# Moving matrix transposes from the tensor engine to DMA in a linear-attention-plus-MLP kernel, with a reordered load and a second load gate

## The chip, the cores and the metric

The kernel runs on one core of one Trainium2 chip. The metric is the device time of one execution in microseconds (us), for the slowest core (here the only one). Executions of one kernel on this chip usually agree within a few tenths of a per cent (the kernel before: 290.83 to 291.37 us in the 20 runs of two groups; in a third group one run of 11 took 292.80 us), so a kernel is timed several times, in rounds that alternate with the kernel before. Engines are named as in the profile: PE is the tensor engine's matmuls, PEld its weight loads (they overlap PE: 158.9 us busy beside PE's 279.8 in a span of 289.2 us), DVE the vector engine, ACT the scalar engine, POOL the general engine (it issues the loads here), SP the sync engine (it issues stores and DMA transposes here).

## The reference, cut to what matters

```python
# q, k, v: [8 batches, 8 heads, 576 rows, 64]
kv  = einsum('bhsd,bhse->bhde', k, v)            # one 64x64 matrix for each batch and head
out = einsum('bhsd,bhde->bhse', q, kv)
x   = out / sqrt(mean(out**2, -1) + 1e-6) * g_norm   # over the 64 of a head
x   = x.transpose(0, 2, 1, 3).reshape(8, 576, 512)
# layer norm, MLP 512 -> 2048 -> 512, residual
xn  = (x - mean(x)) / sqrt(var(x) + 1e-6) * g_ln
return x + maximum(xn @ w_ch1, 0) @ w_ch2
```

## The kernel before

All matmuls are in bf16. A batch of 576 rows is four "main" tiles of 128 rows and a rest of 64 rows; the rests of two batches make one tile more. For each tile the kernel computes q times kv, normalises the result to x on ACT and DVE, turns x (the MLP needs it with d_model on the partitions), and runs the two products of the MLP, mm1 (`w1`) and mm2 (`w2`). Both q and x have to be turned. Where time is short they are turned by four PE matmuls against the identity, into PSUM, with a copy by ACT; elsewhere one DMA does it.

```python
def load_batch(b, after=None):
    if after is not None:
        nc.gpsimd.tensor_copy(gate, after)     # POOL waits for one element: holds the loads back
    load(k_in[b % NB], k, b)                   # two DMAs each, 256 KB and 320 KB
    load(v_in[b % NB], v, b)
    load(q_in[b % NB], q, b)

def turn_q(b, j, pool, tag):                   # one of the five groups of q, on PE
    tp = pool.tile([128, HP, 128], bf16, tag=tag, name="tp")
    for hp in range(HP):
        nc.tensor.transpose(tp[:, hp, :n], q_ps[b][:n, j, ...], identity[:n, :n])
    nc.scalar.copy(qts[b][:, j, :, :n], tp[:, :, :n])

def turn_q_dma(b):                             # all five groups, by DMA (batches 2 to 7)
    q_p = kv_in.tile(...)
    nc.vector.tensor_copy(q_p.rearrange("p j h d -> p h j d"), q_in[b % NB])
    q_t = qt_pool.tile(...)
    nc.sync.dma_start_transpose(q_t..., q_p...)
    qts[b] = q_t

def kv_of(b):                                  # k^T v: 40 small matmuls
    ...
```

The MLP's matmuls are cut into slots, and an agenda says at which slot other work is put between them: `at(slot, function)`; `tick()` in the MLP loops advances the slot and runs what is due. One slot is about 0.86 us of matmuls: late in the kernel before, with nothing between them, the 16 slots of mm2 of a batch took 13.82 us (244.02 to 257.84 us). Slots 0 to 15 are mm1 of batch 0, 16 to 31 mm2 of batch 0, 32 to 47 mm1 of batch 1, and so on. `plan_tile(s, make, turn_at, on_pe)` plans a tile's attention at slot s and the turning of its x at slot turn_at, on PE or by DMA.

```python
load_w2(0); load_w2(1)
load_batch(1)
load_w2(2); load_w2(3)
...
fill(18)                                       # matmuls on zeros while the first loads come in
...
at(21, lambda: kv_of(1))
q_turns(23, 1)                                 # batch 1: copy of q, then turn_q of all 5 groups on PE
for j, s, tn in ((0, 24, 30), (1, 27, 34), (2, 31, 38), (3, 35, 42)):
    plan_tile(s, lambda j=j: main_tile(1, j), tn, True)
at(36, lambda: kv_of(2))
at(36.5, lambda: turn_q_dma(2))
for j, s, tn in ((0, 44, 50), (1, 48, 54), (2, 53, 61), (3, 58, 67)):
    plan_tile(s, lambda j=j: main_tile(2, j), tn, j > 1)      # tiles 2 and 3 on PE
for b in range(3, B):
    s = 32 * b
    at(47 if b == 3 else s - 60,
       lambda b=b: load_batch(b, qts[b - 1][:1, J, HP - 1, 127:]))  # not before q of b-1 is turned
    d = -41 if b == 3 else -45
    at(s + d, lambda b=b: kv_of(b))
    at(s + d + 1.7, lambda b=b: turn_q_dma(b))
    for j in range(J):
        o = s + d + (10 if b == 3 else 13) + 5 * j
        plan_tile(o, lambda b=b, j=j: main_tile(b, j), o + 6, False)
    ...
```

The cut places are marked with dots.

## Time and profile before

The kernel before takes 290.84 us (median of three runs, 290.82 to 290.87). What matters of its profile:

| | before |
|---|---|
| span of the profiled execution | 289.2 us |
| PE busy | 279.8 us, 97% of the span |
| ACT and DVE busy | 155.4 and 149.8 us |
| chain that ended last | 91% PE |
| transposes on PE of batch 1's q, of x by single tiles | 20 and 32 matmuls |

The page's first lines give the span, the busy time of each engine with its number of instructions, and the shares of the chain that ended last, by engine and by line of the kernel:

```profile
span 289.2 us, 5765 instructions
...
PE 279.8 (97%) x2289; PEld 158.9 (55%) x2315; DVE 149.8 (52%) x331; ACT 155.4 (54%) x338; POOL 40.9 (14%) x68
...
PE 91%; DMA 2%; DVE 2%; ACT 2%; issue 1%; DVEq 0%; POOLq 0%
```

PE has almost no idle time, and the chain is PE. Only less PE work, or a shorter pause of PE, can save time. The list of PE's waits has, for each line and cause, the sum in us, the number of waits and the longest one:

```profile
PE even L224 <- DMA v_in<-in_v_dram: 1.5, 1, 1.5
PE p L197 <- DVE eps_sb L137: 1.2, 1, 1.2
PE p L428 <- issue: 1.0, 6, 0.2
PE tp L553 <- DVE xc L546: 0.4, 1, 0.4
```

The waits at L224, L197 and L553 are in the start-up; after it PE waits for no data at all. The timeline of PE in the middle of mm2 of batch 0 has start, length, line and operation:

```profile
41.36 0.38 PE L170 MATMUL tp<-identity,q_p 128*128 128x128 bf16 x4
41.58 1.03 PE L428 MATMUL p<-w_sb,m 128*128 128x512 bf16 x4
42.67 0.38 PE L170 MATMUL tp<-identity,q_p 128*128 128x128 bf16 x4
```

Matmuls overlap in these records, so a transpose's own length is not its cost. The four transposes push the next MLP matmul back by 0.22 us (41.36 to 41.58), and more where they also wait for a PSUM buffer: the next two groups of q push the matmuls after them back by 0.45 and 0.32 us (to 42.89 and 44.07, less a slot of 0.86 us each), since they start at 42.67 and 43.85 us, after the ACT copies of the groups before them, 0.58 us each, had ended at 42.62 and 43.67.

### The profile page before, as it was taken

The numbers are of one execution on the slowest core, as the hardware profiler recorded it, in microseconds if no ns is written. First come the engines' busy times: TensorE is split into PE (matmuls) and PEld (weight loads), VectorE is DVE, ScalarE is ACT, GpSimd is POOL, SyncE is SP. The second block draws the span as 40 slices with busy tenths as digits, with TensorE's granted clock in tenths as the row PEclk, the third lists the DMA queues.
The fourth block names the chain that finished last, engine by engine and source line by source line (L and its number), as shares of the span: only waits on it lengthen the run. The fifth ranks groups of instructions, "written<-read, shape, count | busy, mean of one in ns | idle before, by whom it ended". The sixth has DMA issues, their size and how long they took to land.

```text
span 289.2 us, 5765 instructions
## 1 busy us (share of the span) xinstructions
PE 279.8 (97%) x2289; PEld 158.9 (55%) x2315; DVE 149.8 (52%) x331; ACT 155.4 (54%) x338; POOL 40.9 (14%) x68
## 2 busy tenths in 40 slices
PE   7889999999999999999999999999999999999995
PEld 3579755995569644445444444444444444444444
DVE  5774028838987783765366925762578300220022
ACT  3477854985469832882288418920894076016500
POOL 8522520031032003200410022000000000000000
PEclk9999999999999999999999999999999999999999
DMA  7999999569999929996997179937202510131033
GB/s 215 199 208 202 201 203 206 125 103 196 151 168 129 178 53 165 184 164 123 144 211 102 39 146 204 170 79 161 54 18 54 111 36 0 39 82 27 0 74 73
DMA packets 64890, 36.10 MB, mean 125 GB/s; under 512 B 32860, under 2 KB 59868, under 8 KB 64864
## 3 DMA queue, kind: packets, MB, share of 16 engines
q0 software_dynamic: 28528, 17.76, 46.0%
q1 hardware_dynamic: 35824, 17.25, 31.3%
q10 hardware_dynamic: 512, 0.72, 0.7%
q8 instruction: 18, 0.29, 0.4%
q14 instruction: 8, 0.07, 0.1%
HBM read 36.71 MB, written 9.44 MB: 160 GB/s over the span
## 4 chain that ended last, share of the span: by engine, by line
PE 91%; DMA 2%; DVE 2%; ACT 2%; issue 1%; DVEq 0%; POOLq 0%
PE p L428 43%; PE p L412 42%; PE o_ps L270 3%; DMA v_in<-in_v_dram 2%; PE kv_ps L245 2%; ACT m L415 1%; DVE x_blk L288 0%; DVE xc L546 0%; PE tp L347 0%; ACT sq L276 0%; ACT xT_blk L349 0%; PE tp L170 0%; ACT rms L307 0%; DVE ss L512 0%; PE tp L553 0%
## 5 line engine op out<-in xcount | busy, mean ns | idle before, releaser
L412 PE MATMUL p<-xT_blk,w_sb 128*128 128x128 bf16 (+2 forms) x1017 | 131.4, 285 | 0.8
L428 PE MATMUL p<-w_sb,m 128*128 128x512 bf16 (+2 forms) x590 | 126.8, 368 | 1.6 <-issue 1.0
L415 ACT ACTIVATE m<-p 128x512 bf16<-128x512 f32 x144 | 85.4, 596 | 43.9 <-PE p L412 41.8
L412 PEld LDWEIGHTS <-w_sb 128*128 128x128 bf16 x1024 | 78.6, 98 | 44.5 <-issue 1.1
L428 PEld LDWEIGHTS <-m 128*128 128x128 bf16 x608 | 56.8, 98 | 61.7
L433 DVE SCALAR_TENSOR_TENSOR o_sb<-p,rstd,x_blk 128x512 f32<-128x512 f32 (+2 forms) x38 | 27.3, 721 | 53.2 <-PE p L428 47.6
L276 ACT ACTIVATE sq<-o_ps 128x512 f32<-128x512 f32 x35 | 20.9, 596 | 42.1 <-PE o_ps L270 42.1
L297 DVE TENSOR_REDUCE ss<-sq 128x8 f32<-128x512 f32 x35 | 23.7, 678 | 11.4 <-ACT sq L276 11.4
L339 ACT ACTIVATE dev<-x_blk,st_blk 128x512 f32<-128x512 f32 x36 | 25.7, 714 | 4.6 <-DVE st_blk L325 4.4
L331 DVE SCALAR_TENSOR_TENSOR xc<-x_blk,st_blk,g_ln_sb 128x512 bf16<-128x512 f32 x34 | 25.6, 752 | 1.2
L302 DVE TENSOR_TENSOR y<-o_ps,inv 128x512 f32<-128x512 f32 x33 | 22.8, 692 | 3.0
L321 DVE SCALAR_TENSOR_TENSOR x_blk<-y,g_norm_sb 128x512 f32<-128x512 f32 x33 | 22.8, 692 | 1.1
L314 DVE RECIPROCAL inv<-rms 128x8 f32<-128x8 f32 x36 | 7.2, 201 | 24.8 <-ACT rms L307 24.8
L421 DVE RECIPROCAL rstd<-rstd 128x4 f32<-128x4 f32 x9 | 1.6, 174 | 34.7 <-ACT rstd L420 34.7
L98 POOL COPY gate<-qt 1x1 bf16<-1x1 bf16 x5 | 0.9, 176 | 113.2 <-DMA qt<-q_p 113.2
L307 ACT ACTIVATE rms<-ss,eps_sb 128x8 f32<-128x8 f32 x36 | 10.7, 297 | 8.0 <-DVE ss L297 7.7
L270 PEld LDWEIGHTS <-qt 128*128 128x128 bf16 (+1 forms) x156 | 10.2, 100 | 7.3 <-issue 1.7
L270 PE MATMUL o_ps<-kv_pack,qt 128*128 128x128 bf16 (+1 forms) x156 | 13.7, 220 | 0.1
L197 PE MATMUL p<-fill_sb 128*128 128x512 bf16 x26 | 7.8, 449 | 1.3 <-DVE eps_sb L137 1.2
L339 ACT ACTIVATION_READ_ACCUMULATOR dev<-x_blk,st_blk 128x1 f32 x36 | 6.9, 190 | 0.0
L248 ACT CAST kv_pack<-kv_ps 64x256 bf16<-64x256 f32 x7 | 2.6, 365 | 7.2 <-PE kv_ps L245 7.2
L245 PEld LDWEIGHTS <-k_in 128*64 128x64 bf16 x280 | 5.0, 112 | 2.6 <-issue 2.5
(79 smaller groups left out, 116.5 us busy)
## 6 DMA issues: line engine op xcount, KB each, us to landing
out_dram<-o_sb SPq DMA_DIRECT2D x70, 128.0 KB, 2.4
w_sb<-in_moe_w_ch_dram POOLq DMA_DIRECT2D x8, 512.0 KB, 14.0
k_in<-in_k_dram POOLq DMA_DIRECT2D x7, 320.0 KB, 5.8
v_in<-in_v_dram POOLq DMA_DIRECT2D x7, 320.0 KB, 10.2
q_in<-in_q_dram POOLq DMA_DIRECT2D x7, 320.0 KB, 13.0
q_in<-in_q_dram POOLq DMA_DIRECT2D x8, 256.0 KB, 13.3
k_in<-in_k_dram POOLq DMA_DIRECT2D x7, 256.0 KB, 7.4
v_in<-in_v_dram POOLq DMA_DIRECT2D x7, 256.0 KB, 11.0
```

What stands on the lines that cost most here:

```text
L245: nc.tensor.matmul(kv_ps[hh * D:hh * D + D, hp, :], lhsT=k_in[b % NB][:, h, j, :], rhs=v_in[b % NB][:, h, j, :], start=(j == 0), stop=(j = ...
L270: nc.tensor.matmul(flat[rows, hp * 128:(hp + 1) * 128], lhsT=lhsT_of(hp), rhs=kvp[:, hp, :], start=True, stop=True)
L276: nc.scalar.activation(self.sq_t, self.o_ps, func=AF.Square)
L297: nc.vector.tensor_reduce(self.ss, self.sq_t, axis=AX.X, op=ALU.add)
L302: nc.vector.tensor_mul(self.y_t, self.o_ps, self.inv().to_broadcast([128, H, D]))
L321: nc.vector.scalar_tensor_tensor(x_blk[:, ts].rearrange("p (h d) -> p h d", h=H), in0=self.y_t, scalar=1.0, in1=g_norm_sb.to_broadcast([12 ...
L331: nc.vector.scalar_tensor_tensor(self.xc_t, in0=x_blk[:, self.ts], scalar=st[:, 1, self.ts:self.ts + 1], in1=g_ln_sb, op0=ALU.add, op1=ALU ...
L339: nc.scalar.activation(dev, x_blk[:, ts], func=AF.Square, bias=st[:, 1, ts:ts + 1], accum_out=st[:, 2, ts:ts + 1])
L412: nc.tensor.matmul(p1[:, i, :], lhsT=w1_sb[:, kk, de * 128:(de + 1) * 128], rhs=blk[2][:, kk, sl], start=(kk == 0), stop=(kk == nK - 1))
L415: nc.scalar.activation(m1[:, de0:de0 + per, sl], p1, func=AF.Relu)
L428: nc.tensor.matmul(p2[:, c0:c1], lhsT=m1s[b][:, de, ts * 128:(ts + 1) * 128], rhs=w2_sb[:, de, c0:c1], start=(de == 0), stop=(de == nDe - 1))
L433: nc.vector.scalar_tensor_tensor(o_sb[:, c0:c1], in0=p2[:, c0:c1], scalar=rstds[b][:, ts:ts + 1], in1=blks[b][0][:, ts, c0:c1], op0=ALU.mu ...
```

## The change

The intent is to take transposes off PE, the engine that is the limit, and give them to DMA. It has three parts. First, batch 1's q is loaded before its k and v, so that it can be copied early and three of its five groups can be turned by one DMA while the other loads run; only two groups stay on PE. Second, tiles 2 and 3 of batch 2's x are turned by DMA. The slots of batch 2's tiles, and of batch 3's by one, move to make room (batch 1's k-v product also goes from slot 21 to 22, since its v now comes last), and a second gate keeps batch 4's loads back until tile 3 has been turned, so that the loads don't slow it (in the kernel before, such transposes landed in 9.7 and 10.4 us among batch 4's loads, and in 2.5 us alone). Third, the copy of batch 2's q is asked for at slot 36.9 rather than 36.5.

```diff
-    def load_batch(b, after=None):
-        if after is not None:
-            nc.gpsimd.tensor_copy(gate, after)
+    def load_batch(b, *after):
+        for element in after:
+            nc.gpsimd.tensor_copy(gate, element)
...
-    load_batch(1)
+    for dst, src in ((q_in, q), (k_in, k), (v_in, v)):
+        load(dst[1], src, 1)
...
-    def q_turns(s, b):                # all five groups on PE
-        ...
-    at(21, lambda: kv_of(1))
-    q_turns(23, 1)
+    def q_start():
+        q_ps[1] = kv_in.tile([128, JJ, H, D], bf16, tag="qp", bufs=2, name="q_p")
+        nc.vector.tensor_copy(q_ps[1].rearrange("p j h d -> p h j d"), q_in[1])
+        qts[1] = qt_pool.tile([128, JJ, HP, 128], bf16, tag="qt", name="qt")
+        nc.sync.dma_start_transpose(
+            qts[1][:, 2:].rearrange("p j hp t -> p (j hp) t"),
+            q_ps[1][:, 2:].rearrange("p j h d -> p (j h d)"))
+    def q_turns():
+        turn_q(1, 0, ps_out, "ops")
+        turn_q(1, 1, ps_m, "misc")
+        del q_ps[1]
+    at(14.5, q_start)
+    at(19, q_turns)
+    at(22, lambda: kv_of(1))
...
-    at(36.5, lambda: turn_q_dma(2))
-    for j, s, tn in ((0, 44, 50), (1, 48, 54), (2, 53, 61), (3, 58, 67)):
-        plan_tile(s, lambda j=j: main_tile(2, j), tn, j > 1)
+    at(36.9, lambda: turn_q_dma(2))
+    for j, s, tn in ((0, 45, 51), (1, 49, 55), (2, 53, 61), (3, 57.5, 64)):
+        plan_tile(s, lambda j=j: main_tile(2, j), tn, False)
...
-           lambda b=b: load_batch(b, qts[b - 1][:1, J, HP - 1, 127:]))
+           lambda b=b: load_batch(b, qts[b - 1][:1, J, HP - 1, 127:],
+                                  *([blks[2][2][:1, nK - 1, 511:]] if b == 4 else [])))
...
-            o = s + d + (10 if b == 3 else 13) + 5 * j
+            o = s + d + (11 if b == 3 else 13) + 5 * j
```

More of the change, by code (lines that the diff above doesn't have):

```diff
@@ L602 @@
     at(20, lambda: (rstd_of(0), t.clear()))
-    def q_turns(s, b):
-        def start():
-            q_ps[b] = kv_in.tile([128, JJ, H, D], bf16, tag="qp", bufs=2, name="q_p")
-            nc.vector.tensor_copy(q_ps[b].rearrange("p j h d -> p h j d"), q_in[b % NB])
-            qts[b] = qt_pool.tile([128, JJ, HP, 128], bf16, tag="qt", name="qt")
-            turn_q(b, 0, ps_out, "ops")
-            turn_q(b, 1, ps_m, "misc")
-        at(s, start)
-        for i, j in enumerate((2, 3, 4)):
-            at(s + 1.5 + i, lambda j=j: turn_q(b, j, ps_m, "misc"))
-        at(s + 4, lambda: q_ps.pop(b))
-    at(21, lambda: kv_of(1))
-    q_turns(23, 1)
+    def q_start():
[12 more added lines that the diff above has]
+    at(22, lambda: kv_of(1))
     for j, s, tn in ((0, 24, 30), (1, 27, 34), (2, 31, 38), (3, 35, 42)):
```

## The prediction

This was written before the changed kernel had run.

> **What bounds the kernel.** The tensor engine: on the page PE is busy 279.8 of 289.2 us (97%), clock 1.0; the chain that ended last is 91% PE, 85% in the two MLP products (L412, L428). PE's waits total 4.1 us (list of waits), most in the first 8 us. Time goes only if PE work or a PE pause goes; a new pause costs its length.
>
> **Removed.** By the order of instructions, 20 PE transposes and their PSUM copies on ACT: 12 of q (groups 2, 3, 4 of batch 1), 8 of x (tiles 2, 3 of batch 2). In the timeline four transposes push the next matmuls back by 0.22 us (79.0, 85.3 us). The three q groups cost 0.22, 0.45 and 0.32 us: two also paused, as the one "misc" buffer was not yet freed by the ACT copy (0.58 us). That is 1.0 us for q and 0.44 us for x: 1.4 us, all on the chain. Freed ACT time is worth nothing: ACT is 54% busy, off the chain.
>
> **Added and moved.** One DMA transpose of 12 blocks (393 KB), two of 4 blocks, one POOL gate. PE work moved by a tick changes no sum. The third part (batch 2's q copy at 36.9 instead of 36.5) leaves DVE's order around it as it was: worth nothing.
>
> **What may be given back: DMA.** [...] one x transpose lands in 2.5 us alone (110 us), in 9.7 to 10.4 us among batch 4's loads (86 to 95 us).
>
> 1. From 14 to 50 us loads run at 200 GB/s without a gap. q of batch 1 takes k's old slots, lands at about 31.4 us, is copied by 32.3 us; its transpose then joins the loads and should delay those behind by 1 to 2 us[...]. v of batch 1 would land at 37.2 us plus that, needed near 38.6; the third quarter of w2 at 39.6 us plus that, needed near 41.4. Stall: 0 to 0.6 us.
> 2. Batch 2 tile 3: its transpose stands in SP's queue behind batch 1's last stores, issues near 85 us, lands near 88; needed near 89. Probably no stall.
> 3. The new gate holds batch 4's loads until then: they start near 88.5 us instead of 84.6. From first issue until v landed took 9.3 us (batch 3) and 13.0 us (batch 4), so v lands at 98 to 101.5 us, needed near 99.3. Stall: 0 to 2 us, the likeliest loss.
>
> **Sum.** 290.84 - 1.4 + about 0.4 (expected stalls) = 289.8 us; 289.1 to 291.2 should hold it 8 times in 10. Faster by over 2%: 0.01; within: 0.97; slower: 0.02.
>
> **What would show it.** Groups: q transposes x8 for x20, x transposes x24 for x32. Chain and waits: PE waiting for v_in near 38 us, w_sb near 41, xT near 89, v_in near 99, each with its length. DMA: the new q transpose lands in 4 to 10 us.
>
> **What would make it wrong.** v of batch 4 past 103 us; DVE held by a q copy whose load is late, so that PSUM buffers come free late; or a hidden pause that the change removes elsewhere.

## The result, and the profile after

The changed kernel takes 290.98 us (median of four fast runs, 290.53 to 291.66); the kernel before took 290.86 us in the same rounds. The ratio is 1.0006, with a 95% interval of 0.9982 to 1.0031: no difference. Here and below, a ratio is the mean time of one kernel's fast runs over that of the other's of the same rounds, so it is not quite the ratio of the medians quoted. Below, "ratio" is always against the kernel before. A run counts as slow when it is over 1.5% above the fastest of its kernel; all others are called fast.

The first lines of the page, for the changed kernel:

```profile
span 289.9 us, 5728 instructions
...
PE 278.9 (96%) x2270; PEld 158.1 (55%) x2295; DVE 149.8 (52%) x331; ACT 153.0 (53%) x333; POOL 41.2 (14%) x69
...
PE 69%; DMA 19%; issue 9%; POOL 2%; DVE 0%; POOLq 0%
PE p L429 35%; PE p L413 31%; DMA v_in<-in_v_dram 14%; DMA w_sb<-in_moe_w_ch_dram 5%; PE o_ps L271 2%; PE kv_ps L246 1%; POOL k_in L93 0%; POOL v_in L93 0%; POOL k_in L94 0%; POOL q_in L94 0%; DVE o_sb L434 0%; POOL gate L98 0%; POOLq L93 0%; POOLq L94 0%; POOLq L690 0%
```

PE is busy 0.9 us less and yet the span is not shorter. The chain shows why to look further: before, it was 91% PE. Now 19% of it is DMA, and the largest such item is the load of v. PE has become late behind the loads. The share tells where the chain ran, not what was lost: the two new waits for v are 1.0 us. The list of PE's waits says where (lines of this kernel are one higher):

```profile
PE even L225 <- DMA v_in<-in_v_dram: 2.0, 1, 2.0
PE p L198 <- DVE eps_sb L137: 1.2, 1, 1.2
PE kv_ps L246 <- DMA v_in<-in_v_dram: 1.0, 2, 0.6
PE p L429 <- issue: 1.0, 6, 0.2
PE tp L554 <- DVE xc L547: 0.4, 1, 0.4
```

The line at L246 is new: two waits of the k-v product for v, 1.0 us together. The timeline gives them, with the idle time before the instruction and its releaser in brackets:

```profile
73.14 0.82 PE L246 MATMUL kv_ps<-v_in,k_in 128*64 128x64 bf16 x40 [0.39 <-DMA v_in<-in_v_dram]
...
101.03 0.82 PE L246 MATMUL kv_ps<-v_in,k_in 128*64 128x64 bf16 x40 [0.61 <-DMA v_in<-in_v_dram]
```

They belong to batches 3 and 4. The transposes went as planned. The lists of the two tiles, restricted to PE's weight loads, have 20 and 32 instructions before:

```profile
L170 PEld LDWEIGHTS <-q_p x20: 93/97/98, 39.6 to 43.9; 128*128 128x128 bf16 x16, 64*128 64x128 bf16 x4
...
L347 PEld LDWEIGHTS <-xc x32: 97/98/98, 21.9 to 85.4; 128*128 128x128 bf16 x32
```

and 8 and 24 after:

```profile
L171 PEld LDWEIGHTS <-q_p x8: 97/98/98, 36.0 to 36.6; 128*128 128x128 bf16 x8
...
L348 PEld LDWEIGHTS <-xc x24: 97/98/98, 22.7 to 60.4; 128*128 128x128 bf16 x24
```

What this was worth is read by cutting the span at landmarks (starts of stages in the timeline of PE, us from the span's start) and comparing stage with stage:

| stretch | before | after | after minus before |
|---|---|---|---|
| start to the first product with v | 8.27 | 9.02 | +0.75 |
| from there to the start of mm2 of batch 0 | 24.64 | 24.65 | +0.01 |
| mm2 of batch 0 | 17.02 | 16.16 | -0.86 |
| mm1 of batch 1 to the k-v product of batch 3 | 22.85 | 23.31 | +0.46 |
| to the k-v product of batch 4 | 27.89 | 27.89 | 0.00 |
| to the last PE instruction | 185.04 | 185.08 | +0.04 |
| last PE instruction to the end | 3.45 | 3.75 | +0.30 |
| sum | 289.16 | 289.86 | +0.70 |

The saving of the q part is there (-0.86 us). The x part's saving (0.44 us by the prediction) is swallowed in the line with 0.00. There the wait for v of batch 4 (0.61 us) takes it back. The rest is a late start, a wait for v of batch 3, and a longer end. The experiments ask which of these belong to the change and which to this one execution. (The profile of after shows a mean clock of 0.997 rather than 1.000. The lower readings, 0.5 from 288.13 us, come only after the last PE work and cost nothing.)

### The profile page after: what moved, and what is told of

Same layout as the page of the kernel before. It is cut to its first block, busy times and chain, and to the rows that moved or that the text cites. A ratio compares the mean times of both kernels' runs of the same rounds, so it can differ in the third digit from the quotient of the medians.

```text
span 289.9 us, 5728 instructions
## 1 busy us (share of the span) xinstructions
PE 278.9 (96%) x2270; PEld 158.1 (55%) x2295; DVE 149.8 (52%) x331; ACT 153.0 (53%) x333; POOL 41.2 (14%) x69
## 4 chain that ended last, share of the span: by engine, by line
PE 69%; DMA 19%; issue 9%; POOL 2%; DVE 0%; POOLq 0%
PE p L429 35%; PE p L413 31%; DMA v_in<-in_v_dram 14%; DMA w_sb<-in_moe_w_ch_dram 5%; PE o_ps L271 2%; PE kv_ps L246 1%; POOL k_in L93 0%; POOL v_in L93 0%; POOL k_in L94 0%; POOL q_in L94 0%; DVE o_sb L434 0%; POOL gate L98 0%; POOLq L93 0%; POOLq L94 0%; POOLq L690 0%
## 5 line engine op out<-in xcount | busy, mean ns | idle before, releaser
L308 ACT ACTIVATE rms<-ss,eps_sb 128x8 f32<-128x8 f32 x36 | 10.7, 296 | 10.6 <-DVE ss L298 10.4
L246 PEld LDWEIGHTS <-k_in 128*64 128x64 bf16 x280 | 5.0, 112 | 3.7 <-issue 3.6
```

Of the source, the lines that this page charges most:

```text
L308: nc.scalar.activation(self.r, self.ss, func=AF.Sqrt, scale=1.0 / D, bias=eps_sb)
```

## The experiments

All eleven kernels other than the changed one were built from one of the two kernels by the edits shown, and all but one compute the right result. Three groups ran. The kernel before took 290.97 us (median of 11 runs), 290.95 us (9 runs) and 290.96 us (11 runs) in them.

The theory was that the savings are real and are paid back at the waits for v of batches 3 and 4 (the loads of batch 4 start later, held by the new gate), so that asking for v later would win them back. Call it the *v theory*. Its rivals were that the q part gives its saving back at once, since its transpose crowds the loads (the *crowding theory*), and that the loss belongs to the load order, or is only scatter between executions (the *order or scatter theory*). A fourth theory came up on the way.

### The changed kernel again (`again`)

No edit.

> The changed kernel unaltered, to see its spread and a second trace. Theory A (the 1.4 us of tensor-engine work is saved; about 1 us comes back as waits for v of batches 3 and 4, and single executions also start up to 0.8 us late because the first load of v lands late, by chance and not by the change): 290.5 to 291.7 us, in a fast trace the product over the first load of v starts at the same time as before, the two later waits for v are there again with 0.3 to 1.0 us together. Rival B (the change itself makes the beginning late): every trace shows the start of the second MLP product of batch 0 at 33.5 us or later, against 32.9 before.

Measured: 290.94 us (median of four fast runs, 290.44 to 291.06), ratio 0.9994 (0.9981 to 1.0007). So the time of the changed kernel is that of before within 0.2%. One execution of this run took 1036.65 us, and it is the one that was profiled, so this run gave no fast trace, and what was expected of one stays unread here. In its trace the first v landed near 8.1 us; in the first trace of the same kernel it landed near 9.0 us. `nogate` and `later2` below, which begin like the changed kernel, start mm2 of batch 0 at 32.90 and 32.87 us, against 32.91 before, so Rival B fails: the late start is no fixed property of the kernel. In the trace of the long execution the MLP matmuls took a mean of 742 and 1057 ns, where 285 and 368 are usual, at a recorded clock of 1.0. It counts as slow, nothing here explains it, and it is left out.

### k-v products and q transposes of batches 3 and 4 one slot later (`later`)

```diff
-        at(s + d, lambda b=b: kv_of(b))
-        at(s + d + 1.7, lambda b=b: turn_q_dma(b))
+        late = 1 if b < 5 else 0
+        at(s + d + late, lambda b=b: kv_of(b))
+        at(s + d + 1.7 + late, lambda b=b: turn_q_dma(b))
```

> The changed kernel with the k-v products of batches 3 and 4 one slot (0.86 us) later, so that v has landed. Theory A: both waits for v vanish or nearly so, nothing new appears, 289.5 to 290.2 us, that is 0.5 to 1.0 us under the changed kernel. Rival C (the saving was never 1.4 us, the waits only fill time that would be lost anyway): no gain beyond 0.2 us.

Measured: 290.76 us (290.56 to 292.38), ratio 1.0000 (0.9981 to 1.0018). The expected gain did not come; this is what Rival C said. The waits for v of batches 3 and 4 are gone, but PE now waits further on, as its list shows:

```profile
PE p L413 <- DMA xT_blk<-xc: 0.3, 1, 0.3
...
PE o_ps L271 <- DMA qt<-q_p: 0.2, 1, 0.2
```

(The first is for x of batch 4, the second for q of batch 3.) The whole branch after the load is late, not v alone: q of the same batch is turned later, and then x. Moving the first consumer moves the wait down the branch. The second half of the v theory fails.

### Only the k-v products of batches 3 and 4 later (`later2`), and the same shift on the kernel before (`before_later`)

```diff
-        at(s + d, lambda b=b: kv_of(b))
+        at(s + d + (1 if b < 5 else 0), lambda b=b: kv_of(b))
```

> The changed kernel with only the k-v products of batches 3 and 4 one slot (0.86 us) later; the copies and DMA transposes of q stay in their slots (the run named later moved them too, and waits for transposed q of 0.3 us and for transposed x of 0.4 us took the place of the waits for v). Theory A: no wait for v, none for q or x; 289.4 to 290.2 us, at least 0.5 us under the changed kernel. Rival C (any slot gained is lost to the next wait): 290.4 to 291 us with a new wait of about 0.5 us in the trace.

Measured: 290.43 us (290.37 to 291.22), ratio 0.9986 (0.9974 to 0.9999). At most a gain of 0.1 to 0.2%, under the 0.5 us that was expected. Here a wait of 0.52 us for v of batch 1 showed up (v landed at 38.93 us), the q part's stall that the prediction had given as 0 to 0.6 us. One wait down the branch of batch 4 remained: 0.29 us for its x.

The control moves both calls, as `later` does, in the kernel before, which waits for no v there:

> Control: the kernel before with the k-v products and q copies of batches 3 and 4 one slot later. Theory A: nothing to gain since nothing waited for v there, 290.7 to 291.3 us. If it gains 0.5 us, the slots and not the waits made the difference. Also a second trace of a kernel that loads k first: the first product over v starts at 8.2 to 9.0 us if the late start is chance, always near 8.3 us if it comes with loading q first.

Measured: 290.94 us (290.84 to 291.04), ratio 0.9998 (0.9984 to 1.0012). Moving the slots is in itself worth nothing.

### Without the second gate (`nogate`)

```diff
-           lambda b=b: load_batch(b, qts[b - 1][:1, J, HP - 1, 127:],
-                                  *([blks[2][2][:1, nK - 1, 511:]] if b == 4 else [])))
+           lambda b=b: load_batch(b, qts[b - 1][:1, J, HP - 1, 127:]))
```

> The changed kernel without the new POOL gate ahead of batch 4's loads. Theory A (the gate is what makes v of batch 4 late, and is needed since transposes among loads land in about 10 us): the wait for v of batch 4 near 101 us vanishes, but the transpose of batch 2's tile 3 lands near 95 us instead of 89 and the tensor engine waits 3 to 6 us for it near 90 us; 293 to 296 us. Rival D (the gate is useless): 0.4 to 0.6 us under the changed kernel.

Measured: 300.25 us (299.1 to 300.64), ratio 1.0311 (1.0294 to 1.0328): 9.3 us slower. The chain has the transpose of tile 3 (start, length):

```profile
85.77 9.48 DMA xT_blk<-xc
```

and the list of PE's waits has it at mm1 of batch 2:

```profile
PE p L413 <- DMA xT_blk<-xc: 6.5, 2, 6.3
```

The gate is needed: among batch 4's loads the transpose takes 9.5 us instead of 2.5. (An instruction fetch, a packet on a queue that the profile calls "instruction", of which more below, fell into it too, from 91.62 to 92.99 us. Two transposes among the same loads with no fetch inside took 7.4 us in the first trace of the changed kernel and 8.4 in `x_only`, so the loads alone cost most of it.) The loss is larger than the 293 to 296 us expected. The waits are 6.5 us of it; and PE's granted clock was 0.5 from 92.57 to 99.40 us, after PE had stood still from 89.02 us, so that from 95.30 to 99.40 us its matmuls ran at half the clock, which is an estimated 2 us more (half of these 4.1 us).

The gate is also the cost of the x part, because it delays the loads by more than their slack. The two timelines of POOL show it, gate and first load of batch 4. Before:

```profile
83.38 0.18 POOL L98 COPY gate<-qt 1x1 bf16<-1x1 bf16 x1 [16.93 <-DMA qt<-q_p]
84.57 0.68 POOL L93 DMA_DIRECT2D k_in<-in_k_dram  x1 [1.01 <-PE o_ps L270]
```

After:

```profile
89.10 0.45 POOL L98 COPY gate<-xT_blk 1x1 bf16<-1x1 bf16 x1 [4.96 <-DMA xT_blk<-xc]
90.28 0.68 POOL L93 DMA_DIRECT2D k_in<-in_k_dram  x1 [0.74 <-PE p L413]
```

The loads start 5.7 us later, v of batch 4 lands at 100.89 us, and PE, which would have reached the k-v product near 100.4 us, waits 0.61 us. In the kernel before, v had landed at 97.60 us, 3.07 us before its product at 100.67; the gate moves the landing by 3.29 us.

### The q part alone (`q_only`)

```diff
-    for j, s, tn in ((0, 45, 51), (1, 49, 55), (2, 53, 61), (3, 57.5, 64)):
-        plan_tile(s, lambda j=j: main_tile(2, j), tn, False)
+    for j, s, tn in ((0, 44, 50), (1, 48, 54), (2, 53, 61), (3, 58, 67)):
+        plan_tile(s, lambda j=j: main_tile(2, j), tn, j > 1)
```

with the second gate taken out and `11` set back to `10`.

> Only the q part: q of batch 1 loaded first, three groups by DMA; x of batch 2 turned as before, no gate, slots of batches 2 and 3 as before. Theory A: 1.0 us saved, no wait for v of batch 4, perhaps 0.4 us for v of batch 3: 289.8 to 290.3 us, faster than the whole change. Rival E (the added DMA transpose costs what it saves, by delaying the loads 2 us or more): 290.7 us or above, with waits for v, w2 or the transposed q between 38 and 50 us.

Measured: 290.60 us (289.95 to 290.87), ratio 0.9981 (0.9969 to 0.9993). The q part is a gain of about 0.2%, or 0.55 us (0.0019 x 290.97). mm2 of batch 0 took 16.01 us instead of 17.02, so its 1.0 us of PE work is fully saved there. The crowding theory, that the q part gives it all back, fails. The gain is less than the 0.7 to 1.2 us that was expected; the profiled execution had the late start, 0.65 us.

### The x part alone (`x_only`)

The kernel before with the second gate, batch 2's new slots and transposes by DMA, and `11` for `10`; batch 1 as before.

> The kernel before with only the x part: tiles 2 and 3 of batch 2 turned by DMA, their slots, batch 3's slots, and the gate ahead of batch 4's loads. Theory A: 0.44 us saved, 0.5 to 0.8 us lost in a wait for v of batch 4 near 101 us: 290.8 to 291.3 us, no gain over the kernel before. Rival (the x part gains, the q part is what wastes): 290.4 us or below, no wait for v.

Measured: 293.90 us (293.53 to 294.22), ratio 1.0100 (1.0086 to 1.0113). This was a miss: it is 3 us slower than either kernel. The list of waits:

```profile
PE kv_ps L245 <- DMA v_in<-in_v_dram: 1.6, 1, 1.6
...
PE p L412 <- DMA xT_blk<-xc: 1.0, 1, 1.0
```

With the same gate and the same slots as the changed kernel, the transpose of tile 3 was issued at 86.46 us and landed at 90.79, in 4.3 us instead of 2.5. No load ran beside it. The view of DMA from 87.5 to 90 us shows something else on the rings (queue and kind: packets, MB, share of the 16 engines):

```profile
q1 hardware_dynamic: 566, 0.17, 91.9%
q8 instruction: 1, 0.02, 3.5%
```

One packet of 16,384 bytes on a queue of kind "instruction" was under way from 87.86 to 89.25 us. The transposes' packets that started between 88.31 and 88.62 us all ended together near 90.02 us. The table of windows, asked for SP so that no busy time of other engines stands in it, has the stretch, its length, PE's clock, the DMA share and GB/s (a share over 1 comes of packets whose times overlap):

```profile
87.00:88.00 1.00, 1.00 0.94 199
88.00:89.00 1.00, 1.00 1.83 81
89.00:90.00 1.00, 1.00 0.07 7
90.00:91.00 1.00, 1.00 0.67 129
```

From 89 to 90 us next to no packet was started (the table books a packet where it starts). This suggested a new theory, the *fetch theory*: an instruction fetch that falls into a DMA transpose holds it for over a microsecond. The author took these packets for PE's own instructions, which no view shows as such: the page of before lists 18 packets on that queue, 0.29 MB in all, and PE has 2289 + 2315 recorded instructions, about 256 for each packet. If so, where a fetch falls in time depends on how many PE instructions stand before it. The changed kernel and `x_only` differ in this number, by the 12 transposes of q. The next three experiments test it.

### x_only with fewer filler matmuls (`x_neg`)

```diff
-    fill(18)
+    fill(12)
...
-    fill(1)
...
-    dead = fill(3)
...
-    fill(5, dead)
-    del dead
```

Fifteen fewer matmuls and weight loads in the start-up bring the count of PE instructions before the transpose close to that of the changed kernel.

> The x part alone, as in x_only (293.9 us), with 15 filler matmuls at the start left out (they compute nothing), so that the tensor engine's instruction stream is 30 instructions shorter ahead of batch 2. Theory F (in x_only the 16 KB fetch of instructions at 87.9 us falls into the transpose of batch 2's tile 3, holds every packet in flight for 1.6 us, and so costs 1.2 us at that tile and more at v of batch 4): the fetch moves to about 89.5 us, behind the landing, the wait for x near 90 us vanishes, the wait for v of batch 4 falls below 0.9 us, 290.7 to 291.7 us. Rival G (the x part is slower by itself when the tensor engine is not held up earlier): 293.5 us or above with the same two waits. A start slower by up to 0.4 us, or a lower clock at the start, would be the price of fewer fillers.

Measured: 293.09 us (292.91 to 295.11), ratio 1.0078 (1.0046 to 1.0111). The total is no clean test, because fewer fillers cost something themselves: mm2 of batch 0 began 1.43 us later than in `x_only`, and the granted clock was 0.5 from 8.80 to 19.04 us, where `x_only` had 1.0. So the expected 290.7 to 291.7 us were missed. The stage is a better test; in it the clock was 1.0 in both. The fetch moved to 92.1 us. The transpose landed in 2.52 us (87.90 to 90.42), and the waits shrank:

```profile
PE kv_ps L245 <- DMA v_in<-in_v_dram: 0.4, 1, 0.4
```

From the start of mm2 of batch 0 to the start of mm1 of batch 3 `x_neg` took 80.13 us, `x_only` 82.47 and the kernel before 79.97. So the 2.3 us between the two go with the place of the fetch. The x part with the fetch out of the way is still not below the kernel before in this stretch: the 0.44 us it saves are paid at v of batch 4.

### The changed kernel with the fetch moved into the transpose (`after_shift`), and with q's DMA transpose taken away (`free_q`)

The first adds 21 short instruction pairs net, with nearly the same filler time:

```diff
-    fill(18)
+    early = fill(15)
+    for _ in range(24):
+        nc.tensor.matmul(early[:, :64], lhsT=fill_sb[:, :128], rhs=fill_sb[:, :64],
+                         start=True, stop=True)
+    del early
```

> The whole change with 3 long filler matmuls at the start exchanged for 24 short ones, 42 instructions more ahead of batch 2. Theory F: the fetch moves from 90.1 to about 87.8 us, into the transpose of batch 2's tile 3, which then lands near 91 us; waits of about 1 us for x and over 1 us for v of batch 4; 292.2 to 294.5 us. Rival G: as the changed kernel, 290.4 to 291.7 us.

The second gives a wrong result (relative error 0.26), since three groups of batch 1's q become zero:

```diff
-        nc.sync.dma_start_transpose(
-            qts[1][:, 2:].rearrange("p j hp t -> p (j hp) t"),
-            q_ps[1][:, 2:].rearrange("p j h d -> p (j h d)"))
+        nc.gpsimd.memset(qts[1][:, 2:], 0.0)
```

> The whole change with the DMA transpose of q of batch 1 replaced by a fill with zeros (wrong result on purpose: three of five groups of batch 1): the tensor engine's saving without its DMA cost. Theory A: loads behind it land 1.9 to 2.8 us sooner (v of batch 1 near 37 us, third quarter of w2 near 39.6 us), no wait at the k-v product of batch 1 in any execution, so 0.3 to 0.8 us under the changed kernel: 289.8 to 290.5 us; the wait for v of batch 4 (0.5 to 0.8 us) stays. Rival E' (the DMA transpose costs nothing): as the changed kernel, 290.4 to 291.7 us.

Measured: `after_shift` 292.37 us (291.81 to 294.59), ratio 1.0052 (1.0016 to 1.0088); `free_q` 290.76 us (290.48 to 290.89), ratio 0.9984 (0.9957 to 1.0011). The two happen to be a pair: mm1 of batch 2 starts at 80.92 and 80.91 us, so all before it took equally long. In `free_q` the fetch came at 88.78 us, after the transpose had landed (87.96). In `after_shift` it came at 86.25 to 87.72 us, inside the transpose that was issued at 85.49, and that landed near 89.4, after 3.9 us instead of 2.5. The waits of `after_shift`:

```profile
PE kv_ps L246 <- DMA v_in<-in_v_dram: 1.7, 1, 1.7
...
PE p L413 <- DMA xT_blk<-xc: 0.7, 1, 0.7
```

The wait of `free_q`:

```profile
PE kv_ps L246 <- DMA v_in<-in_v_dram: 0.6, 1, 0.6
```

By mm1 of batch 3 `after_shift` was 1.98 us behind (114.03 against 112.05). The view of DMA from 86 to 88 us has the same transposes in both, with the fetch in `after_shift`:

```profile
q1 hardware_dynamic: 577, 0.26, 76.4%
q8 instruction: 1, 0.02, 4.6%
```

and without it in `free_q`:

```profile
q1 hardware_dynamic: 644, 0.27, 64.7%
```

The fetch theory holds in both directions: with the fetch inside a transpose the loss is there (2.3 us of `x_only` against `x_neg`, 1.98 us of `after_shift` against `free_q`), and with the fetch outside it is not. Neither pair is perfectly clean: `x_neg` also starts later than `x_only`, and `free_q` also lacks the q transpose, which ended some 40 us before. But up to 80.9 us the second pair runs alike to 0.01 us. In the first trace of the changed kernel the fetch came at 90.10 us, one microsecond after the transpose had landed, and it cost nothing. That is luck, not design.

`free_q` also weighs the q transpose's load on DMA. Without it v of batch 1 landed at 37.47 us, in the other kernels with the q part between 38.16 and 39.21. So the transpose does delay the loads behind it by 0.7 to 1.7 us, where 1 to 2 us had been predicted. Yet `free_q` is only about 0.2 us below the changed kernel (290.76 against 290.94 and 290.98), within the scatter and short of the 0.3 to 0.8 us that was expected. So no run shows that more than about 0.2 us of this delay reaches PE.

### Only the load order (`q_first`)

```diff
-    load_batch(1)
+    for dst, src in ((q_in, q), (k_in, k), (v_in, v)):
+        load(dst[1], src, 1)
...
-    at(21, lambda: kv_of(1))
+    at(22, lambda: kv_of(1))
```

> The kernel before with q of batch 1 loaded ahead of its k and v and that k-v product one slot later; all five groups of q turned by the tensor engine as before. Theory A: the order of loads alone costs and gains nothing, 290.7 to 291.2 us. Rival B (loading q first makes the start late or unsteady): spread of 0.7 us or more and a start of the first product over v of 8.6 us or later.

Measured: 290.96 us (290.87 to 291.07), ratio 0.9999 (0.9987 to 1.0012). The load order alone costs nothing, so the load order is not the cause. Its start was early (8.23 us).

### The q part with the k-v product of batch 1 a slot later (`q_kv23`)

```diff
-    at(22, lambda: kv_of(1))
+    at(23, lambda: kv_of(1))
```

> The q part alone (q_only, 290.6 us) with the k-v product of batch 1 one more slot later (23 for 22), so that v of batch 1 has landed in every execution. Theory A: gains what q_only loses there when its start is early, up to 0.6 us, if the third quarter of w2 (lands 41.5 to 42.2 us, needed near 41.4 us) does not take the wait over: 289.9 to 290.5 us. If it does, no gain: 290.3 to 290.9 us, with a wait for w_sb near 41.5 us.

Measured: 290.18 us (290.02 to 291.32), ratio 0.9972 (0.9950 to 0.9995). This is what was expected, and the best median of all: below the kernel before by 0.8 us (0.0028 x 290.96). The list of waits shows none for v other than the one in the start-up. It is a small gain, and its interval overlaps that of `q_only`, so it is shown to be below the kernel before, but not to be below `q_only`.

### Built but not run

The third part of the change, slot 36.9 for 36.5, was taken back alone. The instructions and waits on every engine then come out in the same order, so it can do nothing, and it went to no chip.

### Landmarks of the main traces

All are us from the span's start, from the timeline of PE; the last row is the span less the end of the last PE instruction.

| | before | after | q_only | x_only | x_neg | after_shift | free_q | q_kv23 |
|---|---|---|---|---|---|---|---|---|
| first product with v | 8.27 | 9.02 | 8.92 | 8.19 | 8.12 | 8.20 | 8.19 | 9.21 |
| mm2 of batch 0 | 32.91 | 33.67 | 33.57 | 32.83 | 34.26 | 32.85 | 32.84 | 33.86 |
| mm1 of batch 1 | 49.93 | 49.83 | 49.58 | 49.85 | 51.28 | 48.86 | 48.85 | 49.98 |
| mm1 of batch 2 | 82.22 | 82.34 | 81.86 | 81.91 | 83.34 | 80.92 | 80.91 | 82.47 |
| mm1 of batch 3 | 112.88 | 113.28 | 112.45 | 115.30 | 114.39 | 114.03 | 112.05 | 112.90 |
| last PE instruction | 285.71 | 286.11 | 285.28 | 288.12 | 287.22 | 286.86 | 284.87 | 285.73 |
| from there to the end | 3.45 | 3.75 | 3.55 | 3.83 | 3.79 | 3.74 | 3.84 | 3.53 |

The last row answers for the longer end. In the traces SP checks the eight completion semaphores of its DMAs one after another at the end, 0.06 us each, in a fixed order. In the kernel before two checks remain when the last store has landed; in the changed kernel seven do: five more at 0.06 us are the 0.3 us. Which semaphore the last store has depends on how many DMAs were issued before it, and the change issues three more: SP's DMAs take the eight in turn, and the last store had the seventh in the order of the checks before, the second after. All traces with the x part have an end of 3.72 us or more, and those without it 3.45 to 3.55 us.

## Why the prediction was right or wrong

**What bounds the kernel: right.** PE was the limit; the load order alone (`q_first`) and moved slots (`before_later`) moved nothing.

**1.4 us of PE work removed: right.** The q part's 1.0 us shows as 16.01 us for mm2 of batch 0 in `q_only`, instead of 17.02. The x part's 0.44 us shows between the start of mm1 of batch 1 and the k-v product of batch 4: 51.20 us in the changed kernel, or 50.20 without its 1.00 us of waits for v, against 50.66 in `q_only`, which waits for no v there.

**The third part is worth nothing: right**, by the order of instructions alone.

**"The new q transpose lands in 4 to 10 us": wrong.** It took 15.0 us. The DMA issues of the changed kernel near 32 us (size, us to landing) show that a plain load took no less:

```profile
k_in<-in_k_dram POOLq DMA_DIRECT2D x1, 256.0 KB, 17.4
...
qt<-q_p SPq DMA_TRANSPOSE x1, 15.0
```

The prediction doesn't say how it came to its figure; a load that was issued just before took longer still, so what such an estimate has to count is the queue that is already there. Beside the loads the transpose of 393 KB took no longer than a load of 256 KB (15.0 and 17.4 us), and alone an x tile of 128 KB takes 2.5 us, where the stores of 128 KB take 2.4 us (median, page of before). The q of batch 2, 655 KB with no load beside it, landed in 4.9 us, and DMA moved 216 GB/s while its packets ran (58.5 to 61 us of the changed kernel). The error cost nothing, since three groups are needed late. The delay of the loads behind it (1 to 2 us predicted, where 2 us is 393 KB at the 200 GB/s of the loads and 1 us the author's estimate; 0.7 to 1.7 measured against `free_q`) and the stall at v of batch 1 (0 to 0.6 predicted, 0 to 0.52 measured) were about right.

**Tile 3 of batch 2, "probably no stall": right by luck.** It was issued at 86.45, landed near 89.0 and was needed at 89.8 us; 85, 88 and 89 had been predicted. But the margin is 0.8 us, and an instruction fetch that fell into the transpose made it 1.4 to 1.8 us longer. `x_only` and `after_shift` show that it does fall there when the number of instructions is another. The prediction did not know of this cost.

**The gate: right.** Loads of batch 4 from 88.5 us predicted and 90.28 measured, and PE came to the product near 100.4 us, not 99.3; v landed at 98 to 101.5 predicted and 100.89 measured; "Stall: 0 to 2 us, the likeliest loss" was 0.61 us. `nogate` shows that it can't be left out.

**The sum: too low by 1.2 us.** 289.8 us was predicted and 290.98 measured, inside the range of 289.1 to 291.2. The step that failed is "about 0.4 (expected stalls)", which was too small; the 1.4 us of PE work were right. Three terms make up the 1.4 us that came back:

- The wait for v of batch 4 is 0.6 us (0.61 in the first trace, 0.59 in `free_q`). It was foreseen, though with a smaller weight in the sum. This alone takes back what the x part saves.
- The end of the program is 0.3 us longer. It was not foreseen. It is in every trace with the x part.
- The rest, some 0.5 us, is a remainder that no run isolates. What varies between executions and could make it up: v of batch 1 (0 to 0.52 us), v of batch 3 (0.39 us in the profiled execution, where v took 8.6 us to land instead of 7.2; none in `nogate` and `q_only`), and the late start. These come and go between executions of the same kernel.

So the change is, as far as the runs resolve it, two changes that cancel. The q part gains about 0.5 us (0.9981). The x part seems to lose about as much (the changed kernel, with both, is at 0.9994 and 1.0006): in the traces its 0.44 us are outweighed by 0.6 us at v of batch 4 and 0.3 us at the end. The gain is shown by run times. The loss is read from the traces: the intervals of `q_only` (0.9969 to 0.9993) and `again` (0.9981 to 1.0007) overlap, so the run times alone do not show it.

**What stays open.** The late start (first product with v at 8.66 to 9.21 us rather than about 8.2) came in four of eight traces of kernels with q's DMA transpose, and in none of six without. The loads issued up to that point are the same, and of the changed kernel's two traces one had it and one, that of the long execution, did not. No run shows a cause. The execution of 1036 us is not explained. And the fetch theory is shown by timing alone: what holds the transpose while a fetch is under way was not observed.

## What to carry to other kernels

Work moved from the limiting engine to DMA was worth its PE time here only where the loads behind it had slack (the q part took 1.0 us off PE and gained 0.55 us; the x part's 0.44 us met a wait of 0.6 us for v of batch 4): follow a gate or a delayed load to its next consumer, and do not count on winning by moving that consumer: here the rest of its branch was late too. When a change has independent parts, time them alone: here a gain of 0.2% could not be seen in the whole change, and the first part with one slot moved had the best median. Here a DMA transpose with 0.8 us of margin lost 1.4 to 1.8 us when an instruction fetch fell into it, and the place of the fetch moved with the number of PE instructions (42 more: from 88.78 us in `free_q` to 86.25 in `after_shift`; 30 fewer: from 87.86 us in `x_only` to 92.1 in `x_neg`, 1.43 us of it the later start), so look at where the fetches lie before you trust one trace.
